# A newly searched order of the steps behind the first MoE product, in a fused scan and MoE kernel

## The chip, the cores and the metric

The kernel runs on one core of a Trainium2 chip. The metric is the device time of one execution in microseconds. In the text PE is the tensor engine (PEld its weight loads), DVE the vector engine, ACT the scalar engine, POOL the GpSimd engine, SP the sync engine, which issues nearly all transfers here. PSUM is the memory into which PE writes, SBUF the working memory.

## The reference

Two parts follow each other. The first is a gated state-space scan over `x` (4 batches, 8 heads, 768 positions, 32 wide), with decay `a` and the projections `B` and `C` (16 states). The second is a feed-forward layer over its 3072 tokens of 256 values, with 2048 inner values and a tanh-GELU. All inputs and the output are float32.

```
for each chunk of the sequence:
    cum    = cumsum(log(clip(a)))
    M      = (C B^T) * exp(cum_i - cum_j), lower triangle
    y      = M x  +  (C state) * exp(cum)
    state  = exp(sum) * state + sum_j B_j x_j exp(cum_end - cum_j)
out = gelu_tanh(y_as_tokens @ w_in) @ w_out        # 256 -> 2048 -> 256
```

## The kernel before

The sequence is cut into 24 chunks of 128 positions (six for each batch). Two chunks are a unit `u`, so there are 12 units of 256 tokens. The whole program is a set of named steps, each with a fixed engine. The text `ORDERED` names every step once, and the program issues them in exactly this order. An engine works through its own steps in the order of the text and waits only where data or a buffer isn't ready. A letter behind a colon moves a step to another engine (`:A` ACT, `:D` DVE, `:P` POOL, `:S` SP), `~n` and `+n` put n blocks of matmuls with zeros in a place where PE would stand still.

The steps of a unit or a chunk, with the lines that the profile gives:

- `load_*` (SP): `load_wi.q`, `load_wo.q` bring quarters of the weights, `load_bc.b.i` the B and C of batch b (i = 1 is C), `load_bc1.i` those of chunks 4 and 5, `load_x.u` the x of a unit. `wi.q.k` and `wo.q.k` (line 325 on POOL, 327 on DVE, 323 on ACT) convert the weights to bf16.
- `R`, `tp2`, `tp6.q`, `recip1`, `recip.1.4` (DVE; lines 340, 351, 383, 391) make the decay factors of chunks 4 and 5, and of batches 1 to 3; `pe`, `pp`, `pend` (lines 394 to 396, 402) the factors between chunks.
- `mul1.i` (line 444), `T1.i` (452), `bh1`, `ce1.e` (461), `N1` (472), `bn1` prepare B and C of chunks 4 and 5: scaling, transposing on PE, evicting. For batch 1 these are `mul.1.i` (484), `T.1.i` (493), `E.1.i`, `F.1` (two instructions, 523), `N.1` (529) and `bn.1`. For batches 2 and 3 the transposing goes through DRAM (`load_wr`, `load_tr`, `load_bn`), and only `mul.b.i` and `F.b` remain.
- `G.u` (603) gives the products C B^T of a unit in two PSUM pairs `ga`, `gb`; `M.u.0` and `M.u.1` (613, DVE) mask `ga` and `gb` into `m`. `castx.u` converts x. `D.u` (636) gives the state's increments into a buffer of the pool `hp`; `S.u.k` (682, 684, DVE) adds them to the state, and `SP.c` (691, DVE) spreads the state of chunk c for PE.
- `Y.u` (658, 667) gives y in the PSUM bank `yb`; `yev.u` evicts it into `xm`. From unit 3 on `Y.u` also holds `D` and `G` of the unit behind it.
- `s1.u.i` (717, PE) is an eighth of the first MoE product: four matmuls into one of the two `hp` buffers. `gelu.u.i` (721, ACT) empties that buffer. `s2.u.k.q` (735, PE) is a quarter of the second product for half a unit: four matmuls into the one bank `o_ps` (for a few chunks at the end into `yb`). `oev.c` (323 on ACT, 327 on DVE) evicts chunk c, and `store.c` writes it.

Limits that tie the order together are the buffers: two of `hp` (shared by `s1`, `D`, `pp`), one `o_ps`, one `ga`, one `gb`, one `yb`, six for outputs. `ga` holds the transposed B in its second bank too, so `G` waits until `bn1` or `bn.1` has emptied it:

```
        tn[1].takes("gb", e1)
        tn[0].takes("ga", e0)
        nn.takes("ga", bb)
```

Of the kernel before, what the change touches and what calls it, by code (L numbers as in the profile page):

```python
# [32 lines left out]
s1.2.6 M.3.0 gelu.2.5 wo.3.0:D gelu.2.6 s2.0.0.2.o castx.4.None s1.2.7 Y.3 gelu.2.7 wo.3.1:D
s2.0.1.2.o S.4.0 yev.3.0.2 S.4.1 s2.0.0.3.o oev.0 load_x.5 s1.3.0 s1.3.1 mul.2.1 s2.0.1.3.o
load_wr.2.1 load_x.6 gelu.3.0 gelu.3.1 s1.3.2 oev.1:D SP.8 s1.3.3 s2.1.0.0.o gelu.3.2 M.4.0
gelu.3.3 SP.7 s2.1.0.1.o s2.1.0.2.o s2.1.0.3.o oev.2:D s1.3.4 s1.3.5 s2.1.1.0.o gelu.3.4 M.4.1
mul.2.0:P castx.5.None:A s2.1.1.1.o Y.4 S.5.0 s2.1.1.2.o load_wr.2.0 s2.1.1.3.o load_tr.2.1
load_bn.2 oev.3:D gelu.3.5 s1.3.6 s1.3.7 s2.2.0.0.o yev.4.0.2 load_tr.2.0 gelu.3.6 s1.4.0 SP.9
M.5.1 gelu.3.7 s2.2.0.1.o store.0 store.2 gelu.4.0 s1.4.1 castx.6.None:A s1.4.2 SP.10 s2.2.0.2.o
load_x.7 s2.2.0.3.o gelu.4.1 oev.4:D gelu.4.2 s1.4.3 s1.4.4 load_bc.3.1 s2.2.1.0.o s2.2.1.1.o  # L40
s2.2.1.2.o gelu.4.3 gelu.4.4 s2.2.1.3.o s1.4.5 oev.5 s1.4.6 gelu.4.5 M.5.0 s2.3.0.0.o F.2 store.1
Y.5 s2.3.0.1.o s2.3.0.2.o yev.5.0.2 gelu.4.6 s2.3.0.3.o s1.4.7 S.6.0 gelu.4.7 load_bc.3.0 S.6.1
store.3 s1.5.0 oev.6:D SP.12 s2.3.1.0.o gelu.5.0 s1.5.1 s2.3.1.1.o gelu.5.1 castx.7.None:A
mul.3.1:P s2.3.1.2.o s1.5.2 gelu.5.2 M.6.1 s2.3.1.3.o s1.5.3 M.6.0 Y.6 oev.7:D S.7.0 gelu.5.3
load_x.8 s1.5.4 S.7.1 s2.4.0.0.o s2.4.0.1.o s1.5.5 SP.13 gelu.5.4 load_wr.3.1 yev.6.0.2
castx.8.None store.4 load_x.9 gelu.5.5 SP.14 s2.4.0.2.o s2.4.0.3.o oev.8 s1.5.6 s1.5.7 mul.3.0
castx.9.None s2.4.1.0.o gelu.5.6 load_wr.3.0 gelu.5.7 M.7.0 s2.4.1.1.o s1.6.0 M.7.1 load_tr.3.1
Y.7 S.8.0 load_tr.3.0 gelu.6.0 s1.6.1 s1.6.2 s2.4.1.2.o gelu.6.1 yev.7.0.2:D gelu.6.2 s2.4.1.3.o
oev.9:D M.8.0 s1.6.3 gelu.6.3 SP.16 s1.6.4 s2.5.0.0.o s1.6.5 gelu.6.4 gelu.6.5 M.8.1 SP.15
s2.5.0.1.o s1.6.6 load_bn.3 s2.5.0.2.o s1.6.7 gelu.6.6 s2.5.0.3.o s1.7.0 oev.10:D gelu.6.7 s1.7.1  # L50
gelu.7.0 s2.5.1.0.o s1.7.2 store.5 gelu.7.1 s2.5.1.1.o gelu.7.2 s1.7.3 gelu.7.3 s1.7.4 gelu.7.4
store.9 F.3 s2.5.1.2.o s1.7.5 s1.7.6 gelu.7.5 s2.5.1.3.o s1.7.7 gelu.7.6 store.6 Y.8 oev.11
yev.8.0.2:D gelu.7.7 S.9.0 load_x.10 s2.6.0.0.o s2.6.0.1.o s2.6.0.2.o S.9.1 s1.8.0 gelu.8.0
s2.6.0.3.o s1.8.1 gelu.8.1 oev.12:D s1.8.2 gelu.8.2 s2.6.1.0.o castx.10.None:D store.10 store.11
store.7 s1.8.3 gelu.8.3 s2.6.1.1.o s1.8.4 gelu.8.4 s1.8.5 s2.6.1.2.o s2.6.1.3.o SP.18 M.9.1
gelu.8.5 s1.8.6 M.9.0 store.8 oev.13 gelu.8.6 Y.9 store.12 s2.7.0.0.o s2.7.0.1.o S.10.0 s2.7.0.2.o
yev.9.0.2:D s2.7.0.3.o S.10.1 s1.8.7 oev.14 s1.9.0 load_x.11 castx.11.None:A gelu.8.7 M.10.0
s2.7.1.0.o s2.7.1.1.o SP.21 s1.9.1 s2.7.1.2.o s2.7.1.3.o gelu.9.0 SP.20 gelu.9.1 oev.15 s1.9.2
M.10.1 SP.19 gelu.9.2 Y.10 s1.9.3 gelu.9.3 store.15 S.11.0 s1.9.4 M.11.0 s2.8.0.0.o s1.9.5
gelu.9.4 store.14 s2.8.0.1.o gelu.9.5 s2.8.0.2.o SP.22 s2.8.0.3.o s1.9.6 store.13 gelu.9.6  # L60
oev.16:D s1.9.7 gelu.9.7 yev.10.0.2:D s2.8.1.0.o s1.10.0 s2.8.1.1.o s1.10.1 gelu.10.0 s1.10.2
s2.8.1.2.o gelu.10.1 s1.10.3 s2.8.1.3.o M.11.1 oev.17:D gelu.10.2 s1.10.4 store.17 gelu.10.3
s1.10.5 Y.11 yev.11.0.2:D gelu.10.4 s2.9.0.0.o s1.10.6 gelu.10.5 s2.10.0.0.yb s2.9.0.1.o
s2.10.0.1.yb s1.10.7 s2.10.0.2.yb s2.9.0.2.o gelu.10.6 s2.9.0.3.o s1.11.0 gelu.10.7 s1.11.1 oev.18
s2.9.1.0.o gelu.11.0 store.16 s2.10.0.3.yb s1.11.2 s2.9.1.1.o oev.20 gelu.11.1 s2.9.1.2.o
gelu.11.2 s1.11.3 s2.9.1.3.o gelu.11.3 oev.19:D s1.11.4 s1.11.5 s2.11.0.0.yb gelu.11.4 s1.11.6
gelu.11.5 s2.10.1.0.o store.20 s1.11.7 gelu.11.6 s2.11.0.1.yb s2.10.1.1.o s2.10.1.2.o store.19
s2.10.1.3.o gelu.11.7 oev.21:D s2.11.0.2.yb s2.11.0.3.yb s2.11.1.0.o oev.22:D s2.11.1.1.o store.22
# [915 lines left out]
```

## Time and profile before

| | |
|---|---|
| time, median of 3 runs | 118.44 us (117.72, 118.44, 118.59) |
| profiled execution, span from first to last instruction | 116.9 us |
| what the runs' median has beyond that span | 1.5 us |
| granted TensorE clock in the profile | 1.000 |
| PE, ACT, DVE, POOL busy | 110.1, 72.1, 69.4, 21.4 us |
| first MoE matmul, last MoE matmul | starts at 12.5 us, ends at 113.9 us |
| read from and written to HBM | 11.04 MB, 3.93 MB |

The profile shows one execution; the profiler gives its span alone, and its own time with what lies around the span is not among the three runs. Ends of matmuls are modelled: a group of four that takes PE 0.44 us is shown with 0.60, because the last one outlasts its slot. Gaps between PE's groups are therefore read from starts. A row of the timeline holds start, length, engine, line, operation, output and inputs with their shapes, and a count of merged instructions; brackets hold the idle time of the engine ahead of it and who ended it.

### The profile page before, as it was taken

The numbers are of one execution on the slowest core, as the hardware profiler recorded it, in microseconds if no ns is written. First come the engines' busy times: TensorE is split into PE (matmuls) and PEld (weight loads), VectorE is DVE, ScalarE is ACT, GpSimd is POOL, SyncE is SP. The second block draws the span as 40 slices with busy tenths as digits, with TensorE's granted clock in tenths as the row PEclk, the third lists the DMA queues.
The fourth block names the chain that finished last, engine by engine and source line by source line (L and its number), as shares of the span: only waits on it lengthen the run. The fifth ranks groups of instructions, "written<-read, shape, count | busy, mean of one in ns | idle before, by whom it ended". The sixth has DMA issues, their size and how long they took to land.

```text
span 116.9 us, 3379 instructions
## 1 busy us (share of the span) xinstructions
PE 110.1 (94%) x1426; PEld 92.0 (79%) x1426; DVE 69.4 (59%) x140; ACT 72.1 (62%) x139; POOL 21.4 (18%) x38
## 2 busy tenths in 40 slices
...
PEclk9999999999999999999999999999999999999999
...
GB/s 26 228 332 357 281 252 178 208 288 257 305 143 90 185 47 219 213 253 200 72 25 171 121 163 63 0 140 98 40 6 63 71 0 52 43 0 50 45 47 132
DMA packets 43007, 15.97 MB, mean 137 GB/s; under 512 B 36657, under 2 KB 41457, under 8 KB 42993
## 3 DMA queue, kind: packets, MB, share of 16 engines
...
q8 instruction: 11, 0.18, 0.6%
q10 hardware_dynamic: 192, 0.13, 0.5%
...
HBM read 11.04 MB, written 3.93 MB: 128 GB/s over the span
## 4 chain that ended last, share of the span: by engine, by line
PE 75%; DMA 8%; DVE 6%; SPq 6%; issue 2%; POOL 1%; ACT 0%; DVEq 0%; POOLq 0%
PE o_ps L735 33%; PE hp L717 30%; DMA bcf<-in_B_dram 8%; PE yb L735 3%; SPq L190 3%; PE ga L603 3%; PE yb L658 2%; DVE m L613 2%; PE yb L667 2%; DVE ce L523 1%; SPq L150 1%; DVE bh L327 1%; DVE bc L484 1%; SPq L159 1%; SPq L183 1%
## 5 line engine op out<-in xcount | busy, mean ns | idle before, releaser
L721 ACT ACTIVATE gT<-hp 128x512 bf16<-128x512 f32 x96 | 54.3, 596 | 25.0 <-PE hp L717 24.6
L717 PE MATMUL hp<-xm,w_in_sb 128*128 128x256 bf16 x384 | 53.3, 273 | 0.6 <-ACT gT L721 0.4
L735 PE MATMUL o_ps<-w_out_sb,gT 128*128 128x256 bf16 x352 | 47.3, 273 | 0.0
L717 PEld LDWEIGHTS <-w_in_sb 128*128 128x128 bf16 x384 | 41.4, 114 | 3.5 <-issue 1.9
L735 PEld LDWEIGHTS <-gT 128*128 128x128 bf16 x384 | 37.0, 98 | 4.9 <-issue 1.1
L327 DVE COPY o_sb<-o_ps 128x256 f32<-128x256 f32 x13 | 5.5, 425 | 23.8 <-PE o_ps L735 20.4
L613 DVE TENSOR_TENSOR m<-ga,tri 128x1024 bf16<-128x1024 f32 x12 | 14.6, 1218 | 0.1
L613 DVE TENSOR_TENSOR m<-gb,tri 128x1024 bf16<-128x1024 f32 x11 | 13.4, 1219 | 0.7 <-PE gb L603 0.7
L323 ACT ACTIVATE o_sb<-o_ps 128x256 f32<-128x256 f32 x9 | 3.5, 385 | 9.2 <-PE o_ps L735 9.2
L705 PE MATMUL yb<-wz 128*128 128x512 bf16 (+3 forms) x23 | 7.6, 481 | 1.1 <-DVE wz L220 1.1
L691 DVE SCALAR_TENSOR_TENSOR sp_new<-s_new,pend,bmask 128x256 bf16<-128x256 f32 x17 | 7.9, 476 | 0.0
L327 DVE CAST xm<-yb 128x512 bf16<-128x512 f32 x6 | 4.1, 687 | 5.8 <-PE hp L636 4.8
L684 DVE SCALAR_TENSOR_TENSOR s_new<-s_new,pend,hp 128x64 f32<-128x64 f32 x13 | 3.6, 279 | 6.4 <-PE hp L636 6.2
L705 PEld LDWEIGHTS <-wz 128*128 128x128 bf16 x26 | 3.0, 120 | 5.1 <-issue 3.2
L667 PE MATMUL yb<-m,x 128*32 128x128 bf16 x192 | 6.1, 220 | 0.0
L603 PE MATMUL ga<-ce,bh 32*128 32x256 bf16 x48 | 4.7, 273 | 1.3 <-DVE bn L327 0.9
L484 POOL TENSOR_TENSOR bc<-bc_t,pt 128x768 bf16<-128x768 f32 x2 | 3.0, 1494 | 13.8 <-DMA bc_t<-in_C_dram 13.7
L658 PE MATMUL yb<-ce,sp_new 128*32 128x128 bf16 x160 | 5.3, 221 | 0.0
L603 PE MATMUL gb<-ce,bh 32*128 32x256 bf16 x48 | 4.7, 273 | 0.0
L735 PE MATMUL yb<-w_out_sb,gT 128*128 128x256 bf16 x32 | 4.6, 273 | 0.0
L667 PEld LDWEIGHTS <-x 128*32 128x32 bf16 x192 | 3.8, 97 | 0.8 <-issue 0.8
L323 ACT ACTIVATE xm<-yb 128x512 bf16<-128x512 f32 x6 | 3.6, 595 | 1.1 <-PE hp L636 1.1
...
## 6 DMA issues: line engine op xcount, KB each, us to landing
...
```

What stands on the lines that cost most here:

```text
L323: nc.scalar.activation(o, i, AF.Copy)
L327: nc.vector.tensor_copy(out=o, in_=i)
L484: (nc.gpsimd if eng == "POOL" else nc.vector).tensor_tensor(out=d["bc16"][:, i], in0=d["bc"].rearrange("p i h (r n) -> p i r h n", r=R6)[: ...
L603: nc.tensor.matmul(out=gbank(g)[:, 256 * k:256 * k + 256], lhsT=bh_of(2 * u + k)[gs], rhs=ce_of(2 * u + k)[gs], start=True, stop=True, til ...
L613: nc.vector.tensor_tensor(out=m_of(u)[:, 2 * i:2 * i + 2].rearrange("p g k e t -> p (g k e) t"), in0=gx[i].rearrange("p g (k t) -> p (g k) ...
L658: nc.tensor.matmul(out=y4[32 * j:32 * j + 32, k, w], lhsT=sp[:, 32 * h:32 * h + 32], rhs=ce_of(gc)[:, h % 2], start=first(j), stop=False, ...
L667: nc.tensor.matmul(out=y4[32 * j:32 * j + 32, k, w], lhsT=X16[u][:, k, 32 * h:32 * h + 32], rhs=m[:, h // 2, h % 2, :], start=first(j), st ...
L691: nc.vector.scalar_tensor_tensor(out=sp_new.rearrange("p (g d) -> p g d", g=4), in0=(XN[0][:, H * D:H * D + 64] if gc == 0 else state[("s" ...
L705: nc.tensor.matmul(out=t[:, 0:m * 128], lhsT=wz, rhs=w3.to_broadcast([128, m, 128]), start=True, stop=True, skip_group_check=True)
L717: nc.tensor.matmul(out=hp[:, j * T:(j + 1) * T], lhsT=w_in_k[:, w, q, k], rhs=xm[:, w, u * T:(u + 1) * T], start=(w == 0), stop=(w == 1))
L721: nc.scalar.activation(gts[u][:, 2 * i:2 * i + 2], hps.pop((u, i)).rearrange("p (j t) -> p j t", j=2), AF.Gelu_apprx_tanh)
L735: nc.tensor.matmul(out=ops[gc], lhsT=gts[u][:, fi, k * Q:(k + 1) * Q], rhs=w_out_sb[:, fi, :], start=(fi == 0 and (u > 0 or k == 0)), stop ...
```

## The change

Only the text `ORDERED` is altered. The set of steps is the same. All steps as far as `s1.0.0` stay as they are, apart from `c_wz`, which is named ahead of four loads on other queues. The order of the transfers on SP, stores among them, is the same name for name. Behind `s1.0.0` the order on PE, DVE, ACT and POOL is new, and 38 steps are on another engine. The ten filling blocks of `s1.1.3+10` are left out. Core of the diff:

```diff
-load_aq.0 load_aq.1 load_aq.2 load_aq.3 c_wz load_bc0.1 c_ident c_m4 c_sel c_tri c_zero load_bc0.0
+c_wz load_aq.0 load_aq.1 load_aq.2 load_aq.3 load_bc0.1 c_ident c_m4 c_sel c_tri c_zero load_bc0.0
...
-load_wi.3 S.1.0 s1.0.0 SP.1 xn.2 load_bc1.1 wi.2.0 gelu.0.0 G.1 s1.0.1 s1.0.2 M.1.1 M.1.0
-load_bc1.0 load_wo.0 wi.3.0:D gelu.0.1 wi.2.1 s1.0.3 load_x.2 SP.2 pe wi.3.1 gelu.0.2 load_bc.1.1
-gelu.0.3 tp6.2 s1.0.4 load_bc.1.0 gelu.0.4 load_x.3 load_wo.1 xn.3 s1.0.5 s1.0.6 Y.1 gelu.0.5 pp
-tp2 gelu.0.6 tp6.3 recip1 s1.0.7 S.1.1 yev.1.0.2 mul1.0:P mul1.1:P tp6.1 pend gelu.0.7 s1.1.0
-wo.0.1 T1.0 s1.1.1 T1.1 gelu.1.0 bh1 N1 gelu.1.1 s1.1.2 tp6.0 s1.1.3+10 bn1 ce1.1 load_wo.2
-castx.2.None SP.3 wo.0.0 ce1.0 gelu.1.2 gelu.1.3 G.2 s1.1.4 recip.1.4 s1.1.5 gelu.1.4 M.2.1
-mul.1.1:P s2.0.0.0.o D.2 M.2.0 load_x.4 gelu.1.5 s2.0.1.0.o s1.1.6 T.1.1 gelu.1.6 S.2.0 s1.1.7
-SP.4 Y.2 mul.1.0 yev.2.0.2:D gelu.1.7 wo.1.0 wo.1.1 T.1.0 E.1.1:A castx.3.None:A s1.2.0 wo.2.0
-s1.2.1 E.1.0 wo.2.1 load_wo.3 load_bc.2.1 N.1 gelu.2.0 F.1 s1.2.2 bn.1:D G.3 gelu.2.1 gelu.2.2 D.3
...
+S.1.0 s1.0.0 xn.2 gelu.0.0 load_bc1.1 wi.2.0 G.1 wi.2.1 xn.3 tp2 s1.0.1 M.1.0 s1.0.2 gelu.0.1 recip1
+M.1.1 s1.0.3 wi.3.0 SP.1 mul1.1:P gelu.0.2 s1.0.4 S.1.1 gelu.0.3 gelu.0.4 SP.2 pe T1.1 load_bc1.0
+s1.0.5 tp6.3 wi.3.1 load_wo.0 s1.0.6 Y.1 ce1.1 mul1.0:P gelu.0.5 gelu.0.6 load_x.2 pp T1.0 ce1.0:D
+yev.1.0.2 s1.0.7 bh1 pend:D gelu.0.7 s1.1.0 tp6.1 tp6.0 tp6.2 N1 s1.1.1 bn1:D wo.0.1 G.2 gelu.1.0
+load_bc.1.1 gelu.1.1 s1.1.2 castx.2.None wo.0.0 s1.1.3 gelu.1.2 recip.1.4 mul.1.1:P M.2.1 gelu.1.3
+load_bc.1.0 s1.1.4 s2.0.0.0.o M.2.0 gelu.1.4 D.2 T.1.1 s1.1.5 S.2.0 SP.3 gelu.1.5 s1.1.6 SP.4
+load_x.3 E.1.1 Y.2 mul.1.0:P T.1.0 s1.1.7 load_wo.1 gelu.1.6 yev.2.0.2:D gelu.1.7 s2.0.1.0.o s1.2.0
+s1.2.1 E.1.0 N.1 F.1 wo.1.0:A gelu.2.0 wo.1.1 s2.0.0.1.o bn.1:D gelu.2.1 s1.2.2 castx.3.None:D
+gelu.2.2 load_wo.2 load_x.4 G.3 D.3 wo.2.0 S.3.0 s2.0.1.1.o wo.2.1:D SP.6 s1.2.3 s2.0.0.2.o S.3.1
+s2.0.1.2.o gelu.2.3 M.3.0 s1.2.4 load_wo.3 s1.2.5 wo.3.0:A wo.3.1 s2.0.0.3.o M.3.1 s2.0.1.3.o
+load_bc.2.1 oev.0:D castx.4.None gelu.2.4 gelu.2.5 s1.2.6 Y.3 oev.1 s2.1.0.0.o gelu.2.6 s2.1.0.1.o
+s2.1.0.2.o yev.3.0.2 SP.7 S.4.0 s2.1.0.3.o M.4.1 S.4.1 mul.2.1:P s1.2.7 oev.2 s1.3.0 s2.1.1.0.o
+s2.1.1.1.o s2.1.1.2.o gelu.2.7 s2.1.1.3.o s1.3.1 oev.3:D M.4.0 gelu.3.0 gelu.3.1 s1.3.2 s2.2.0.0.o
...
+gelu.4.5 oev.7:D s1.4.6 s2.4.0.0.o gelu.4.6 Y.5 S.6.0 load_bc.3.0 store.3 s1.4.7 yev.5.0.2 S.6.1
+mul.3.1 load_x.8 load_wr.3.1 s2.4.0.1.o s1.5.0 mul.3.0:P gelu.4.7 s2.4.0.2.o castx.7.None:D gelu.5.0
+store.4 s1.5.1 gelu.5.1 s2.4.0.3.o s1.5.2 oev.8:D load_x.9 load_wr.3.0 gelu.5.2 s1.5.3 s2.4.1.0.o
...
+gelu.6.2 s1.6.4 gelu.6.3 s2.5.1.3.o gelu.6.4 s1.6.5 castx.8.None gelu.6.5 store.6 oev.11:D Y.7 F.3
+load_x.10 s1.6.6 gelu.6.6 s2.6.0.0.o S.8.0 s1.6.7 store.10 gelu.6.7 yev.7.0.2:D store.11 s2.6.0.1.o
+s1.7.0 s2.6.0.2.o M.8.0 M.8.1 SP.16 s1.7.1 s2.6.0.3.o gelu.7.0 oev.12:D s1.7.2 gelu.7.1 s1.7.3
...
```

Both texts run on in this manner to the last step; the second MoE products come earlier against the first ones in the new order (at `Y.3` three more of them have been issued and one `s1` step less).

More of the change, by code (lines that the diff above doesn't have):

```diff
@@ L33 @@
[L33 to L68, printed above, removed]
@@ L69 @@
-s2.11.1.2.o store.21 s2.11.1.3.o oev.23 store.18 store.23
+load_wi.2 SP.0 ~17 Y.0 wi.0.1:A wi.0.0:A S.0.0 yev.0.0.2 wi.1.1 XX.1 wi.1.0:A R XD.1 S.0.1 load_wi.3
+S.1.0 s1.0.0 xn.2 gelu.0.0 load_bc1.1 wi.2.0 G.1 wi.2.1 xn.3 tp2 s1.0.1 M.1.0 s1.0.2 gelu.0.1 recip1
+M.1.1 s1.0.3 wi.3.0 SP.1 mul1.1:P gelu.0.2 s1.0.4 S.1.1 gelu.0.3 gelu.0.4 SP.2 pe T1.1 load_bc1.0
+s1.0.5 tp6.3 wi.3.1 load_wo.0 s1.0.6 Y.1 ce1.1 mul1.0:P gelu.0.5 gelu.0.6 load_x.2 pp T1.0 ce1.0:D
+yev.1.0.2 s1.0.7 bh1 pend:D gelu.0.7 s1.1.0 tp6.1 tp6.0 tp6.2 N1 s1.1.1 bn1:D wo.0.1 G.2 gelu.1.0
```

30 lines of the change are left out of this document (27 added, 3 removed).

## The prediction

> **What bounds the kernel now.** I read the page's busy times first, then the stages, then the engines' timelines where the stages show idle time. Two lines of the page (busy us, share, instructions; granted TensorE clock in 40 slices):
>
> ```profile
> PE 110.1 (94%) x1426; PEld 92.0 (79%) x1426; DVE 69.4 (59%) x140; ACT 72.1 (62%) x139; POOL 21.4 (18%) x38
> PEclk9999999999999999999999999999999999999999
> ```
>
> Four rows of the stages (stretch, length, busy us of PE, PEld, DVE, ACT, POOL, clock, DMA share, GB/s):
>
> ```profile
> 20.00:25.00 5.00, 4.98 (x54) 3.93 (x55) 4.42 (x7) 3.84 (x9) 3.26 (x4) 1.00 1.13 221
> 25.00:30.00 5.00, 3.82 (x70) 2.81 (x67) 4.64 (x7) 3.89 (x7) 3.07 (x5) 1.00 1.07 298
> 30.00:35.00 5.00, 5.00 (x88) 4.30 (x85) 4.33 (x10) 3.36 (x6) 0.00 (x0) 1.00 0.98 210
> 105.00:110.00 5.00, 5.00 (x49) 4.71 (x47) 0.42 (x1) 3.89 (x8) 0.00 (x0) 1.00 0.18 56
> ```
>
> TensorE is full from 30 us to the end at full clock, so behind 30 us an order can only lose; it can win where PE is not full. In the rows from 25 to 30 us DVE is the fuller engine (4.64 of 5). The timeline says what PE waits for (start, length, instruction, in brackets idle time before it and who ended it):
>
> ```profile
> 28.21 0.60 PE L717 MATMUL hp<-xm,w_in_sb 128*128 128x256 bf16 x4
> 29.69 0.28 PE L603 MATMUL ga<-ce,bh 32*128 32x256 bf16 x2 [0.89 <-DVE bn L327]
> 24.82 0.48 DVE L691 SCALAR_TENSOR_TENSOR sp_new<-s_new,pend,bmask 128x256 bf16<-128x256 f32 x1
> 25.22 0.95 DVE L484 TENSOR_TENSOR bc<-bc_t,rt 128x768 bf16<-128x768 f32 x1
> 26.14 0.69 DVE L327 CAST xm<-yb 128x512 bf16<-128x512 f32 x1
> 26.78 0.96 DVE L327 COPY bh<-ga 128x768 bf16<-128x768 bf16 x1
> 27.65 1.52 DVE L523 TENSOR_SCALAR ce<-ch,par 128x768 bf16<-128x768 bf16 x2
> 29.09 0.54 DVE L327 COPY bn<-ga 128x768 bf16<-128x768 bf16 x1
> ```
>
> G.3 (29.69) is the last long wait of PE, and it waits for an unbroken DVE chain: SP.4, mul.1.0, yev.2, E.1.0, both halves of F.1, bn.1. So the change is worth what it does to the moment of G.3, plus the products that PE has done by then, minus new waits behind it.
>
> **The change part by part.** Moving `c_wz` to the front alters no queue, as it already led DVE. The order on SP is word for word the same, and none of its issues before load_wr.2.1 waits for an engine, so landings up to about 35 us stay. The rest goes into four terms.
>
> *One more product before G.3.* Before G.3 the new order has s2.0.0.1 besides all that stood there. PE takes 0.44 us for four matmuls (the starts 43.13 and 44.01 below are eight apart): **−0.44**. The ten filling blocks of `s1.1.3+10` go; their place is one third matmul row,
>
> ```profile
> 20.62 0.70 PE L705 MATMUL hp<-wz 128*128 128x512 bf16 x3
> ```
>
> 0.54 us if the 0.16 by which a matmul outlasts its slot (0.60 for four slots of 0.44) is taken off. They filled a wait, so I count them as room and not as gain: PE could stand at G.3 at 28.21 + 0.44 + 0.44 − 0.54 = 28.55, about 28.7 with its mode switch. That is the earliest G.3.
>
> *The DVE chain up to G.3.* Rows for what leaves and what comes:
>
> ```profile
> 13.48 1.23 DVE L613 TENSOR_TENSOR m<-gb,tri 128x1024 bf16<-128x1024 f32 x1 [0.17 <-PE gb L603]
> 14.62 1.22 DVE L613 TENSOR_TENSOR m<-ga,tri 128x1024 bf16<-128x1024 f32 x1
> 15.75 0.42 DVE L327 CAST w_in_sb<-wf 128x512 bf16<-128x512 f32 x1
> 16.08 0.48 DVE L691 SCALAR_TENSOR_TENSOR sp_new<-s_new,pendq,bmask 128x256 bf16<-128x256 f32 x1
> 16.93 1.94 DVE L351 STREAM_TRANSPOSE rt<-r_t 32x192 f32<-32x192 f32 x6
> 22.24 1.23 DVE L613 TENSOR_TENSOR m<-gb,tri 128x1024 bf16<-128x1024 f32 x1 [0.55 <-PE gb L603]
> 18.14 0.19 ACT L323 ACTIVATE pend<-hp 128x24 f32<-128x24 f32 x1
> 20.47 0.38 ACT L323 ACTIVATE bn<-ga 128x256 bf16<-128x256 bf16 x1
> 20.73 0.84 ACT L461 ACTIVATE ce<-gb,par 128x256 bf16<-128x256 bf16 x2
> 26.06 0.81 ACT L323 ACTIVATE ch<-gb 128x768 bf16<-128x768 bf16 x1
> ```
>
> Idle time 0.17 and 0.55 goes, because tp2 and then M.1.0 fill the first and M.2.1 stands behind DVE work alone. Off DVE go wi.3.0 (15.75 to 16.08: 0.33) and mul.1.0 (25.22 to 26.14: 0.92). Onto DVE come ce1.0, pend, bn1 and E.1.1. DVE does none of these here; ACT's rows give 0.42, 0.19, 0.38 and 0.81. E.1.1 has the shape of E.1.0, 26.78 to 27.65, so 0.87; a 256-wide eviction takes a DVE slot of 0.34 (43.33 to 43.68 in the last fence and its neighbour's start); so 0.34 + 0.20 + 0.34 + 0.87 = 1.75, bounds 1.5 and 2.0. castx.3, too, but behind bn.1, beside G.3. F.1 is the fourth item. It ran while POOL was casting; F.2, the same two instructions, ran with POOL idle:
>
> ```profile
> 48.73 0.74 DVE L523 TENSOR_SCALAR ce<-ch,par 128x768 bf16<-128x768 bf16 x2
> 27.67 1.29 POOL L325 CAST w_out_sb<-wf 128x512 bf16<-128x512 f32 x2 [0.23 <-DMA wf<-in_moe_w_out_dram]
> ```
>
> In the new order one cast of w_out goes to ACT and one to DVE, so F.1 costs nearer 0.74 than 1.52: −0.78. Sum: −0.72 − 1.25 + 1.75 − 0.78 = −1.00, G.3 at 28.7, just where PE could be.
>
> *POOL in DVE's way.* The three SP (two operands in SBUF) now meet POOL. Rows:
>
> ```profile
> 7.75 8.91 DMA bcf<-in_B_dram
> 12.91 2.04 POOL L325 CAST w_in_sb<-wf 128x512 bf16<-128x512 f32 x3 [0.33 <-DMA wf<-in_moe_w_in_dram]
> 19.80 0.61 POOL L325 CAST w_out_sb<-wf 128x512 bf16<-128x512 f32 x1
> 20.35 0.86 POOL L325 CAST x<-x_t 128x512 bf16<-128x512 f32 x1
> 21.88 1.49 POOL L484 TENSOR_TENSOR bc<-bc_t,pt 128x768 bf16<-128x768 f32 x1
> 20.30 0.43 DVE L691 SCALAR_TENSOR_TENSOR sp_new<-s_new,pend,bmask 128x256 bf16<-128x256 f32 x1
> 35.28 2.01 POOL L484 TENSOR_TENSOR bc<-bc_t,rt 128x768 bf16<-128x768 f32 x1 [5.31 <-DMA bc_t<-in_B_dram]
> 34.99 0.95 DVE L484 TENSOR_TENSOR bc<-bc_t,pt 128x768 bf16<-128x768 f32 x1
> ```
>
> DVE: today SP.1 stands between S.1.0 and the 0.17 of idle, so S.1.0 ends near 13.48 − 0.17 − 0.40 = 12.9. Then tp2 takes 0.9 (four of the six transposes of 16.93), M.1.0 and M.1.1 1.14 each (13.48 to 14.62), recip1 and S.1.1 some 0.2 each (estimates), so SP.1 is due at 16.3 and SP.2 at 16.9. POOL: three casts to 14.95, mul1.1 at 15.2 behind recip1, wi.3.1 then until 16.5, mul1.0 at its landing 16.66 (7.75 + 8.91) until 17.3. So SP.1 meets wi.3.1 with 0.2 left and SP.2 meets mul1.0 with 0.4 to 0.5. M.2.1 is due at 21.7 (22.24 less 0.72, 0.33 and SP.3's slot of 0.36, plus 0.88 for ce1.0, pend and bn1); SP.3, now behind two M and S.2.0, at 24.2; mul.1.1 and mul.1.0 occupy POOL from 21.7 for 2 × 1.49, to 24.7: 0.5 left. What a meeting costs DVE no SP row shows outright. Nothing, by the row at 20.30: 0.43, with a POOL cast from 19.80 to 20.41 in progress, but with its last 0.11 us only. By F.1 against F.2, (1.52 − 0.74)/2 = 0.39 each. At most about 0.7 each, if the pushed chain pushes mul.1.1 too. POOL pays the same way: 2.01 against 1.49 when mul.2.1 was running on DVE first, 0.86 against 0.61 beside SP.3. I take F.1's 0.39, three times: **+1.17**, bounds 0 and 2.0, and G.3 at 29.87, **+0.18** on today's 29.69.
>
> The Trainium skill (SBUF — State Buffer, Who interferes with whom) says that a VectorE instruction with two SBUF inputs and a GpSimd instruction that reads SBUF exclude each other, and that whoever starts first keeps the port for its whole instruction. By that rule the three meetings would cost 0.2 + 0.45 + 0.5 = 1.15, nearly what I took. F.1 and the 2.01 row agree with it; the 20.30 row is no test.
>
> *Behind G.3.* PE must stay full. castx.3 on DVE (0.42, as the 15.75 cast) ends as PE reaches D.3. wo.2.1 on DVE and wo.3.0 on ACT come 0.1 to 0.4 before their products. M.3.1, 0.3 before Y.3; if SP.6 meets POOL this goes. mul.2.1 moves to POOL, which is free when C lands, and is followed there by mul.2.0. mul.3.1 goes from POOL to DVE behind S.6.1, some 3 us later, and load_wr.3.1 blocks store.4 and load_x.9 on SP for that time; by counting 0.44 us steps, the first reader (F.3) and the sixth-next output buffer have over 2 us left. The turns of the one `o_ps` bank are the tightest:
>
> ```profile
> 42.25 1.05 PE L735 MATMUL o_ps<-w_out_sb,gT 128*128 128x256 bf16 x8
> 43.13 1.04 PE L717 MATMUL hp<-xm,w_in_sb 128*128 128x256 bf16 x8
> 44.01 0.60 PE L735 MATMUL o_ps<-w_out_sb,gT 128*128 128x256 bf16 x4
> 43.33 0.42 DVE L327 COPY o_sb<-o_ps 128x256 f32<-128x256 f32 x1 [0.98 <-PE o_ps L735]
> 43.68 0.48 DVE L691 SCALAR_TENSOR_TENSOR sp_new<-s_new,pend,bmask 128x256 bf16<-128x256 f32 x1
> ```
>
> Two s1 steps between, and the eviction ends at 43.75, 0.25 before the bank is written again. The new order uses the same spacing; in it oev.12 alone stands behind a full DVE stretch (F.3, S.8.0, yev.7, M.8.0, M.8.1, SP.16) and comes out level with PE: **+0.05**, bounds 0 and 0.4. The tail (eviction, last store) is unchanged.
>
> *Sum:* −0.44 + 0.18 + 0.05 = −0.21. The profiled span is 116.9, so I forecast 116.7; the median of the runs is 118.44, 1.5 above that span, and the same distance makes **118.2**. Its own range, by 0.3 either way at the meetings and 0.4 of the runs' spread (117.72 to 118.59): 117.6 to 118.8.
>
> **The rivals.**
> *POOL does not hold up DVE.* For it: the 20.30 row. Against it: F.1. Then G.3 comes at 28.7, the gain is 0.99 + 0.44 − 0.05 = 1.38 and the time 117.1.
> *PE becomes late before G.3.* The new order lets PE wait for SP.2 in Y.1, for pend behind tp6.3 and ce1.0 before s1.1.0, and for bn1 behind three transposes (0.5 each) before G.2. Then G.2 comes at 21.3, and 12 steps of 0.44 with about 2.4 for G.2, D.2, Y.2 and eighteen transposes follow: 29.0. If in addition the gelus and SP.3 stop it for 1.2 to 1.4, G.3 comes at 30.3: 118.44 + 0.6 − 0.44 + 0.1 = 118.7. Against it: ACT loses four evictions there.
> *Evictions late on DVE (slower).* oev.3, 6, 7, 8, 12 and 13 are on DVE with two s1 steps to the next writing. From 0.25 us of delay each stops PE. An eviction that meets an M half way is 0.61 late, 0.36 beyond its margin; six make 2.2: 120.4. For it: DVE is handed casts and mul.3.1, and its order was fixed by an estimate. Against it: the same spacing costs nothing at 43.33, and DVE is idle before that.
>
> **How the numbers follow.** Forecast 0.42, POOL harmless 0.20, PE late 0.18, evictions late 0.20. Faster by over 1% (under 117.26; about what a measurement here can tell from no change) needs nearly all of the harmless case: 0.16, and 0.04 from cheaper evictions: 0.20. Slower by over 1% (over 119.62): most of the last rival, 0.18, and 0.04 of unseen waits: 0.22. The rest, 0.58, within 1%. The range reaches from the harmless case less 0.2 to about the middle of the last one: 116.9 to 119.7, with 1 in 10 left out on either side.
>
> **What would show it.** Right: s2.0.0.1 before G.3; G.3 between 29.5 and 30.2; SP.1 to SP.3 longer than 0.48 or late behind POOL; F.1 under 1.0; PE full after 31 us. Wrong: G.3 before 29.2 (POOL harmless), idle PE of over 0.3 us in a stretch behind 35 us with an o_sb eviction as releaser (last rival), or a load that lands over 0.5 us later than it does today.

## The result, and the profile after

After takes 119.12 us in the median (118.49 to 120.68, 22 runs) against 118.45 (117.72 to 119.12, 22 runs) before: ratio 1.0055, 95% interval 1.0034 to 1.0076, so 0.67 us slower where 0.2 less was forecast. That lies in the range and in the band of 1%, but the time went up and not down. The profiled execution of after has a span of 117.8 us and a time of 119.47. Two lines of its page, and five stages (stretch, length, busy us of PE, PEld, DVE, ACT, POOL, granted clock, DMA share, GB/s):

```profile
PE 109.4 (93%) x1423; PEld 91.9 (78%) x1423; DVE 69.6 (59%) x139; ACT 71.5 (61%) x136; POOL 24.4 (21%) x42
PEclk9999999999999999999999999999999999999999
```

```profile
16.00:20.00 4.00, 2.89 (x54) 2.33 (x54) 3.80 (x10) 3.07 (x8) 2.57 (x5) 1.00 0.95 224
20.00:25.00 5.00, 4.16 (x46) 3.21 (x45) 4.91 (x9) 3.23 (x6) 3.17 (x4) 1.00 1.05 193
25.00:30.00 5.00, 4.45 (x73) 3.82 (x72) 5.00 (x9) 3.10 (x6) 2.34 (x3) 1.00 1.01 271
30.00:35.00 5.00, 5.00 (x57) 4.14 (x54) 4.48 (x9) 2.88 (x6) 2.62 (x3) 1.00 1.07 268
105.00:110.00 5.00, 5.00 (x48) 4.73 (x47) 0.43 (x1) 3.41 (x7) 0.00 (x0) 1.00 0.17 56
```

PE is full from 30 us on, as before; DVE is full from 20 to 30 us, where before left it 0.9 us idle. The timeline of after, first the instructions that were to be watched on DVE, then POOL beside them, then PE at its waits and at G.3:

```profile
16.10 0.47 DVE L689 SCALAR_TENSOR_TENSOR sp_new<-s_new,pendq,bmask 128x256 bf16<-128x256 f32 x1
16.68 0.65 DVE L689 SCALAR_TENSOR_TENSOR sp_new<-s_new,pendq,bmask 128x256 bf16<-128x256 f32 x1
17.26 0.56 DVE L392 TENSOR_TENSOR pe<-ac,r_t 64x3 f32<-64x3 f32 x1
17.92 0.50 DVE L394 TENSOR_TENSOR pe<-pe,m 64x24 f32<-64x24 f32 x1
24.92 1.69 DVE L689 SCALAR_TENSOR_TENSOR sp_new<-s_new,pend,bmask 128x256 bf16<-128x256 f32 x2
28.86 1.09 DVE L521 TENSOR_SCALAR ce<-ch,par 128x768 bf16<-128x768 bf16 x2
16.43 0.62 POOL L442 TENSOR_TENSOR bc0s<-bcf,pt 128x256 bf16<-128x256 f32 x1 [0.47 <-DMA bcf<-in_C_dram]
17.00 0.80 POOL L323 CAST w_in_sb<-wf 128x512 bf16<-128x512 f32 x1
17.77 0.62 POOL L442 TENSOR_TENSOR bc0s<-bcf,rt 128x256 bf16<-128x256 f32 x1
24.44 1.50 POOL L482 TENSOR_TENSOR bc<-bc_t,rt 128x768 bf16<-128x768 f32 x1 [0.26 <-DMA bc_t<-in_B_dram]
17.11 0.29 PE L450 MATMUL gb<-ident,bc0s 128*128 128x128 bf16 x2 [1.24 <-POOL bc0s L442]
21.58 0.28 PE L601 MATMUL ga<-ce,bh 32*128 32x256 bf16 x2 [0.47 <-DVE bn L325]
26.27 0.29 PE L656 MATMUL yb<-ce,sp_new 128*32 128x128 bf16 x8 [0.55 <-DVE sp_new L689]
27.00 0.51 PE L491 MATMUL ga<-ident,bc 128*128 128x128 bf16 x6
30.47 0.28 PE L601 MATMUL ga<-ce,bh 32*128 32x256 bf16 x2
```

For comparison, SP.2 and the two instructions of `pe` in the timeline of before:

```profile
16.08 0.48 DVE L691 SCALAR_TENSOR_TENSOR sp_new<-s_new,pendq,bmask 128x256 bf16<-128x256 f32 x1
16.48 0.15 DVE L394 TENSOR_TENSOR pe<-ac,r_t 64x3 f32<-64x3 f32 x1
16.73 0.18 DVE L396 TENSOR_TENSOR pe<-pe,m 64x24 f32<-64x24 f32 x1
```

G.3 comes at 30.47, 0.78 later than before, not 0.18. From G.3 to the end of the last matmul it is 83.70 us against 84.18: the product done ahead is worth its 0.44, and nothing is lost behind G.3. So the matmuls end 0.3 us later (114.2 against 113.9). DVE is held up where POOL runs: SP.2 by 0.17, the two of `pe` by 0.41 and 0.32, SP.3 with SP.4 by 0.81 (1.69 against the 0.88 that the first experiment with a short mul.1.0 shows below), F.1 by 0.35 over F.2's 0.74. SP.3 alone takes 1.30 and ends 0.28 us after POOL's mul.1.0. Together that is 2.06 us on DVE's chain, which would else have reached G.3 at 28.4. Not all of it could have been won: bn.1, the last of the chain, ends at 30.41, and PE, which waited 0.55 us for SP.4 ahead of Y.2, runs from there (26.27) to G.3 without a wait of over 0.2 us, so it would have been the next bound.

The span is 0.9 us longer and the matmuls only 0.3. The rest lies behind the last store's landing: 0.89 us of span before (116.01 to 116.9), 1.40 after (116.36 to 117.76). The waits of SP, from 114 us on, show it in their last line (engine, line, what it waited for: us in total, times, longest). Before:

```profile
SPq L979 <- DMA out_dram<-o_sb: 1.1, 2, 0.7
SPq L979 <- PEq L979: 0.6, 2, 0.4
```

After:

```profile
SPq L977 <- DMA out_dram<-o_sb: 1.1, 2, 0.7
SPq L977 <- PEq L977: 1.1, 2, 0.9
```

These are the program's closing instructions, in which all engines wait for each other. POOL is the late one: its last drain starts at 117.35 in after, 0.38 us after the instruction in front of it has ended; in before that gap is 0.03. What lies between span and time goes the other way, 1.71 us after and 1.96 (median of 137 later runs, 1.77 to 2.12) before. From last landing to the time that makes 3.11 against 2.85: 0.26 us in which no step of the order runs.

### The profile page after: what moved, and what is told of

It is laid out like the page before. It is cut to its first block, busy times and chain, and to the rows that moved or that the text cites. A ratio compares the mean times of both kernels' runs of the same rounds, so it can differ in the third digit from the quotient of the medians.

```text
span 117.8 us, 3373 instructions
## 1 busy us (share of the span) xinstructions
PE 109.4 (93%) x1423; PEld 91.9 (78%) x1423; DVE 69.6 (59%) x139; ACT 71.5 (61%) x136; POOL 24.4 (21%) x42
## 4 chain that ended last, share of the span: by engine, by line
PE 75%; DMA 8%; DVE 5%; SPq 5%; ACT 2%; issue 1%; POOL 1%; ACTq 0%; POOLq 0%
PE o_ps L733 33%; PE hp L715 31%; DMA bcf<-in_C_dram 8%; PE yb L733 3%; SPq L188 3%; PE yb L656 2%; PE ga L601 2%; PE yb L665 2%; DVE m L611 2%; DVE rt L349 1%; DVE sp_new L689 1%; ACT gT L719 1%; SPq L148 1%; SPq L181 1%; SPq L157 1%
## 5 line engine op out<-in xcount | busy, mean ns | idle before, releaser
L689 DVE SCALAR_TENSOR_TENSOR sp_new<-s_new,pend,bmask 128x256 bf16<-128x256 f32 x17 | 8.5, 527 | 0.1
L323 POOL CAST x<-x_t 128x512 bf16<-128x512 f32 x6 | 3.7, 615 | 19.9 <-PE gb L601 17.1
L482 POOL TENSOR_TENSOR bc<-bc_t,rt 128x768 bf16<-128x768 f32 x3 | 4.5, 1496 | 12.7 <-DMA bc_t<-in_B_dram 12.7
L321 ACT ACTIVATE xm<-yb 128x512 bf16<-128x512 f32 x9 | 5.4, 597 | 1.4 <-PE hp L634 1.4
L656 PEld LDWEIGHTS <-sp_new 128*32 128x32 bf16 x160 | 2.9, 96 | 2.4 <-issue 1.4
```

The lines of the kernel that those rows point to most:

```text
L321: nc.scalar.activation(o, i, AF.Copy)
L482: (nc.gpsimd if eng == "POOL" else nc.vector).tensor_tensor(out=d["bc16"][:, i], in0=d["bc"].rearrange("p i h (r n) -> p i r h n", r=R6)[: ...
L656: nc.tensor.matmul(out=y4[32 * j:32 * j + 32, k, w], lhsT=sp[:, 32 * h:32 * h + 32], rhs=ce_of(gc)[:, h % 2], start=first(j), stop=False, ...
L689: nc.vector.scalar_tensor_tensor(out=sp_new.rearrange("p (g d) -> p g d", g=4), in0=(XN[0][:, H * D:H * D + 64] if gc == 0 else state[("s" ...
```

## The experiments

The kernel before ran beside each of them; ratios are to it, with 95% intervals.

**Which half of the order?** Two mixed orders, joined behind D.3.

```diff
 e1: before's text up to D.3, then after's steps in after's order
+... G.3 gelu.2.1 gelu.2.2 D.3 s2.0.0.1.o S.3.0 s2.0.1.1.o SP.6 s1.2.3 s2.0.0.2.o S.3.1 ...
 e2: after's text up to D.3, then before's steps in before's order
+... load_x.4 G.3 D.3 wo.2.0 wo.2.1 load_wo.3 load_bc.2.1 s1.2.3 S.3.0 S.3.1 load_bc.2.0 ...
```

> The old order up to D.3 and the new order behind it (s2.0.0.1 comes right behind D.3; wo.2.0 and wo.2.1 stay on POOL). Theory A (the loss lies ahead of G.3: DVE instructions that read two SBUF operands, and F.1, stand still while POOL reads): G.3 near 29.7 us as in the kernel before, SP.3 under 0.5 us, time within 0.3% of the kernel before. Rival B (the loss lies behind G.3, in the new order of the rest): still slower by 0.5 to 0.7 us. Rival C (late landing of the C of chunks 4 and 5 stops PE at T1.1): as A, since the old front has T1.1 later.

> The new order up to D.3 and the old order behind it. Theory A: G.3 near 30.4 us, SP.3 near 1.3 us, and slower than the kernel before by 0.3 to 0.8 us. Rival B: within 0.2 us of the kernel before. Rival C: as A, with PE idle for over 1 us ahead of T1.1.

e1: 1.0068 (1.0030 to 1.0105). e2: 1.0100 (1.0059 to 1.0141). Both are slower than before. Of e1's 0.7% some 0.3% is the long end of the span that is treated below (3.08 us from the last landing to the time); e2 doesn't have it (2.60). In e2 G.3 is 16.95 us behind G.1, PE waits another 0.4 behind 36 us, and the matmuls from G.3 on take 84.40 us, 0.70 more than after's; why this mixture is worse than the whole new order stays open. In e1 the front is as good as before's, and PE waits behind G.3 instead, for casts of the last quarter of w_out:

```profile
32.84 0.63 ACT L323 ACTIVATE w_out_sb<-wf 128x512 bf16<-128x512 f32 x1 [0.72 <-DMA wf<-in_moe_w_out_dram]
32.88 0.61 POOL L325 CAST w_out_sb<-wf 128x512 bf16<-128x512 f32 x1 [2.86 <-DMA wf<-in_moe_w_out_dram]
33.53 1.03 PE L735 MATMUL o_ps<-w_out_sb,gT 128*128 128x256 bf16 x8 [0.28 <-ACT w_out_sb L323]
```

e6 takes that wait away by loading the quarter one place earlier:

```diff
-... load_x.4 ... load_wo.3 ...
+... load_wo.3 load_x.4 ...
```

> The first experiment's order (old up to D.3, new behind it) with load_wo.3 ahead of load_x.4 on SP. Theory D (behind G.3 the new order uses the last quarter of w_out 2 to 3 us earlier than the old one, and its landing at 30.8 us in the profile of before was an early one): PE's wait ahead of s2.0.0.3, 0.45 us at 33 us in the first experiment, goes, and the time falls by 0.3 to 0.6 us against it, to within 0.3% of the kernel before. If the loss of the first experiment lies elsewhere: no change.

1.0024 (0.9987 to 1.0060). The same product, now without a wait:

```profile
32.48 1.04 PE L735 MATMUL o_ps<-w_out_sb,gT 128*128 128x256 bf16 x8
```

So the new rest uses the last quarter early (32.48 in e6, about 35.1 in before, behind Y.3), at times before it has landed. In the whole new order this doesn't show, because G.3 is late.

**What makes G.3 late?** e3 takes PE's wait before T1.1 (1.24 us above) out of the new order.

```diff
-... SP.2 pe T1.1 load_bc1.0 ... Y.1 ce1.1 mul1.0:P ... pp T1.0 ce1.0:D yev.1.0.2 s1.0.7 bh1 ...
+... SP.2 pe load_bc1.0 ... Y.1 mul1.0:P ... pp T1.1 T1.0 ce1.0:D yev.1.0.2 s1.0.7 ce1.1 bh1 ...
```

> The new order with T1.1 on PE moved behind pp (just ahead of T1.0) and ce1.1 on ACT moved behind yev.1, so that PE does not stop for mul1.1 between s1.0.4 and s1.0.5. Theory A: PE is a microsecond less late at s1.0.5, but DVE sets G.3, so G.3 stays within 0.15 us of 30.4 and the time within 0.2 us of the new order. Rival C: G.3 comes 0.4 us or more earlier and the time falls by 0.4 us or more.

1.0036 (1.0003 to 1.0069): some 0.2 us better than after, which the intervals don't tell from nothing. PE waits at other places in its stead (0.47 us for wi.3.1's cast and 0.47 for `pe`), G.3 is at 30.25, and DVE still meets POOL:

```profile
25.06 1.41 DVE L691 SCALAR_TENSOR_TENSOR sp_new<-s_new,pend,bmask 128x256 bf16<-128x256 f32 x2
```

e9 shortens what SP.3 waits for and leaves the order alone. Its mul.1.0 multiplies a third of its columns, and T.1.0 reads that third three times; the other two thirds of the scaled B are left out.

```diff
-            out=d["bc16"][:, i], ...
+            out=d["bc16"][:, i, 0:k], ...          # k = 2 of 6 for mul.1.0
-            ... in_=bc[:, i, r], identity=ident)
+            ... in_=bc[:, i, r % 2 if (b, i) == (1, 0) else r], identity=ident)
```

> The new order; POOL's mul.1.0 multiplies only a third of its columns (256 of 768), and T.1.0 reads that third three times, so the instruction should take about 0.55 us in place of 1.50 and SP.3 should no longer wait for it. Theory (DVE held up by POOL's reads decides the moment of G.3): SP.3 takes 0.48 to 0.6 in place of 1.30, G.3 comes 0.6 to 0.8 sooner than in the new order (29.7 to 29.9), ratio to before 0.999 to 1.001. Rival (TensorE's own wait before T1.1 and G.2 decides, the DVE wait only lies over it): SP.3 is as short, but G.3 moves by under 0.3 and the ratio stays at 1.004 to 1.007. Where wi.3 and C come late, yev.2 waits for PE and part of the gain goes.

```profile
24.13 0.62 POOL L485 TENSOR_TENSOR bc<-bc_t,rt 128x256 bf16<-128x256 f32 x1
24.91 0.88 DVE L692 SCALAR_TENSOR_TENSOR sp_new<-s_new,pend,bmask 128x256 bf16<-128x256 f32 x2
29.67 0.28 PE L604 MATMUL ga<-ce,bh 32*128 32x256 bf16 x2
```

0.9997 (0.9966 to 1.0027). SP.3 and SP.4 take 0.88 in place of 1.69, G.3 comes 0.80 sooner, and the time is back at before's, with an end of the span as long as after's (3.09 us). Up to SP.3 the two profiles agree: G.2 comes at 21.57 (21.58 in after) and SP.3 starts at 24.91 (24.92). So PE's waits ahead of G.2 are still there, and they did not decide. (mul.1.0 had ended at 25.94 in after and T.1.0 read it at 27.00, so a sooner end of mul.1.0 was no gain by itself.)

e10 does e3 and e9 together.

> As the run before, with T1.1 behind T1.0 and ce1.1 ahead of bh1 as well, so that neither suspected wait is left before G.3. Theory that DVE alone decides: about the same as the run before, 0.998 to 1.001. Rival that each of the two holds the other half: clearly faster than either alone, ratio 0.994 to 0.998, G.3 at 29.2 to 29.5.

1.0014 (0.9976 to 1.0053), no more than e9 alone. G.3 came at 29.44, and now the wait of e1 appears:

```profile
33.75 0.92 PE L736 MATMUL o_ps<-w_out_sb,gT 128*128 128x256 bf16 x7 [0.85 <-ACT w_out_sb L323]
```

Two attempts to take SP.3 out of POOL's way by the order failed. e5 puts SP.3 behind bn1; e7 does that, and lets PE and DVE of the front change places as well; e8 is e7 with load_wo.3 ahead of load_x.4.

```diff
 e5:
-... bn1:D ... recip.1.4 ... S.2.0 SP.3 gelu.1.5 s1.1.6 SP.4 load_x.3 E.1.1 ...
+... bn1:D SP.3 ... recip.1.4 ... S.2.0 E.1.1 gelu.1.5 s1.1.6 SP.4 load_x.3 ...
 e7, besides SP.3 and e3's edit:
-... SP.2 pe ... tp6.3 wi.3.1 ... Y.2 mul.1.0:P T.1.0 s1.1.7 ... yev.2.0.2:D ... E.1.0 N.1 ...
+... SP.2 ... tp6.3 pe ... wi.3.1:A ... mul.1.0:P ... s1.1.7 T.1.0 E.1.0 Y.2 ... yev.2.0.2:A ... N.1 ...
```

> The new order with two steps of DVE moved: SP.3 directly behind bn1, where POOL stands still, and E.1.1 ahead of SP.4, so that both SP run outside mul.1.0. Theory A (POOL blocks DVE): SP.3 falls from 1.0 to 1.3 us to 0.5, SP.4 stays near 0.48, bn.1 ends 0.3 to 0.6 us earlier than in the new order and the time falls by 0.2 to 0.5 us. If SP.3 were long for a cause of its own, it stays over 1 us in its new place.

> The new order with its front freed of what blocked DVE: T1.1 and ce1.1 later as in the third experiment, wi.3.1 on ACT, pe behind tp6.3, SP.3 behind bn1, E.1.1 ahead of SP.4, T.1.0 and E.1.0 ahead of Y.2 and yev.2, and yev.2 on ACT. Theory A: pe, SP.3 and SP.4 at their undisturbed lengths, G.3 0.7 to 1.3 us earlier than in the new order (29.2 to 29.8), time 118.0 to 118.5, at or under the kernel before, less what a late w_out costs (theory D: up to 0.5). Rival B (loss behind G.3): no more than 0.2 us of gain.

> The freed front with load_wo.3 ahead of load_x.4. Theories A and D together: 0.2 to 0.5 us under the freed front, 117.7 to 118.1, faster than the kernel before by 0.3 to 0.6%. Theory A without D: as the freed front.

e5: 1.0072 (1.0029 to 1.0115); e7: 1.0120 (1.0071 to 1.0169); e8: 1.0116 (1.0063 to 1.0169). SP.3 takes 0.48 in the profiles of e5 and e7, and it did not help. e7 shows where its gain went: `pe` was put off, PE waits for it, and DVE then waits for PE.

```profile
18.91 0.37 PE L402 MATMUL hp<-pe,selp 128*128 128x24 f32 x2 [0.92 <-DVE pe L396]
19.44 0.48 DVE L463 TENSOR_SCALAR ce<-gb,par 128x256 bf16<-128x256 bf16 x1 [0.67 <-PE gb L452]
```

e5's profile can't be used for that: it is of an execution of 121.76 us (its median is 119.65), in which the loads came late (wi.3 at 16.7 and C at 17.1, where the others have 13.9 to 15.4 and 14.4 to 16.6). Its loss is not explained. So that SP.3 costs time is shown by e9 alone.

e4 tested F.1 in the old order: both halves of wo.2 go from POOL to ACT.

```diff
-... s1.2.0 wo.2.0 s1.2.1 E.1.0 wo.2.1 ... gelu.2.2 D.3 ... gelu.2.3 ...
+... s1.2.0 s1.2.1 E.1.0 ... gelu.2.2 wo.2.0:A D.3 ... gelu.2.3 wo.2.1:A ...
```

> The old order with the two conversions wo.2.0 and wo.2.1 moved from POOL to ACT (behind gelu.2.2 and gelu.2.3), so that POOL converts nothing while DVE does F.1. Theory A: the halves of F.1 fall from 0.84 and 0.76 us to 0.41 each, G.3 comes 0.6 to 0.75 us earlier (29.0), the time falls by 0.5 to 0.8 us to about 117.8. If F.1 were long for a cause of its own: no change.

```profile
27.49 0.95 DVE L523 TENSOR_SCALAR ce<-ch,par 128x768 bf16<-128x768 bf16 x2
```

0.9980 (0.9948 to 1.0011). F.1 takes 0.95 against 1.52 and G.3 stands 16.1 us behind G.1 against 16.7, but the time is hardly less. The profile of before was an unlucky draw at this place: with the same steps in the same order, e13 and e18 below have G.3 16.3 us behind G.1, and F.1 takes 1.10 in both.

e11 was meant to beat both kernels: e6, with mul.1.0 on POOL and wo.2 on ACT.

```diff
-... SP.4 Y.2 mul.1.0 ... wo.2.0 s1.2.1 E.1.0 wo.2.1 ... gelu.2.1 gelu.2.2 D.3 ...
+... SP.4 mul.1.0:P Y.2 ... s1.2.1 E.1.0 ... gelu.2.1 wo.2.0:A gelu.2.2 wo.2.1:A D.3 ...
```

> A version meant to beat both: the old order up to D.3 with the new one behind it and load_wo.3 ahead of load_x.4 (the run e6), and two items taken off the DVE chain before G.3: mul.1.0 goes to POOL, where it follows mul.1.1 (about 23.4 to 24.9, so SP.4 at 24.8 meets only its end), and both halves of wo.2 go to ACT behind gelu.2.1 and gelu.2.2, so that F.1 meets no cast. Theory: DVE is freed by 0.9 + 0.5, G.3 then hangs on PE alone, 28.3 to 28.7, and the ratio is 0.993 to 0.997. Rival: B's chunk lands later than 24.4, SP.4 waits for POOL and the gain is gone: 0.999 to 1.003; or wo.2 on ACT comes late for s2.0.0.2 and shows as a PE wait at 31 us.

0.9991 (0.9957 to 1.0024). DVE is free as planned (0.83 us idle ahead of yev.2), G.3 is 15.9 us behind G.1, and the time is no better. That led back to the end of the span.

**The end of the span.** e11 has the same 3.11 us between last landing and time as after. In every profile with a long end the late instruction of POOL is the 69th that the trace holds of it. The three positions that occur, and before (us behind the last landing):

```
                  recorded on POOL   late one starts    instruction in front of it ended
before                  65           none in the span   -
e7                      70           69th, at 1.04      0.66
after                   71           69th, at 0.99      0.61
e1                      73           69th, at 0.72      0.33
```

e12 to e14 leave every step alone and add small instructions to POOL at its last step, when it has nothing left to do.

```diff
-            fill(yb, int(w[1:]))
+        if w[0] == "!":                       # "!12" stands at the end of ORDERED
+            for _ in range(int(w[1:])):
+                nc.gpsimd.memset(cz[:, 0, 0, 0, 0:2], 0.0)
```

> The new order with 12 tiny memsets on POOL behind its last step, at about 55 us, where POOL has nothing left to do. They change no other engine. Theory (the 69th recorded instruction of POOL is late, wherever it stands; in the new order it is a drain of the closing sequence): the late place is passed long before the end, the span ends 0.9 us behind the last landing in place of 1.40, the distance from span to time stays at 1.7, and the time falls by 0.4 to 0.5: ratio to before 1.001 to 1.003. Rival (the late drain has to do with what the new order does last): 1.40 stays and the ratio stays at 1.004 to 1.007.

> The kernel before with 6 of these memsets, which bring POOL from 65 recorded instructions to 71, as many as the new order has. Theory: the late place moves into the closing sequence: 1.40 behind the last landing in place of 0.89, distance from span to time 1.7 in place of 2.0, time +0.2: ratio 1.001 to 1.002. Rival: nothing moves, 0.89 and 2.0.

> The kernel before with 16 memsets. Theory: the late place is passed in POOL's idle time: 0.89 behind the last landing and 1.7 from span to time, so 0.3 us less: ratio 0.997 to 0.998. Rival: no change, 0.999 to 1.001.

The new order with 12 more: 1.0002 (0.9973 to 1.0031). The old one with 6: 1.0028 (1.0001 to 1.0054); with 16: 0.9970 (0.9939 to 1.0000). Each moved the way the theory said; the first two lie 0.1% outside the ranges that it gave (1.001 to 1.003 and 1.001 to 1.002), well within the noise. The last line of SP's waits moves with it; the new order with 12:

```profile
SPq L981 <- PEq L981: 0.6, 2, 0.4
```

and the old order with 6:

```profile
SPq L983 <- PEq L983: 1.1, 2, 0.9
```

From last landing to time it is 2.64 in e12, 3.10 in e13 and 2.63 in e14, where after has 3.11 and before 2.85. (e14's profile is of an execution of 120.21 us, with its median at 118.07; only this part of it is used here.) In e12, where POOL's 69th recorded instruction is a memset, it starts 0.06 us behind the one before it, like its neighbours: the lateness shows only where the 69th is one of the closing instructions. e18 repeats e14:

> The kernel of e14 once more. If the 0.3 us are real: ratio 0.996 to 0.999, the span 0.9 us behind the last landing and 1.7 us from span to time. If e14 was an accident of its chip: 0.999 to 1.002.

0.9983 (0.9956 to 1.0010), again with 2.65 behind the last landing. Its F.1:

```profile
27.72 1.10 DVE L524 TENSOR_SCALAR ce<-ch,par 128x768 bf16<-128x768 bf16 x2
```

Three more versions were meant to beat both kernels. e15 is e11 with s2.0.1.0 behind T.1.0, s2.0.0.1 ahead of G.3, and 12 memsets; e16 is e4 with 18; e17 is e16 with mul.1.0 on POOL.

```diff
 e15:
-... gelu.1.5 s2.0.1.0.o s1.1.6 ... T.1.0 E.1.1:A ... bn.1:D G.3 ... D.3 s2.0.0.1.o S.3.0 ...
+... gelu.1.5 s1.1.6 ... T.1.0 s2.0.1.0.o E.1.1:A ... bn.1:D s2.0.0.1.o G.3 ... D.3 S.3.0 ...
```

> A version meant to beat both: the run e11, with s2.0.1.0 moved behind T.1.0 (so that PE has it to do while yev.2 runs, where e11 waits 0.5 us) and s2.0.0.1 ahead of G.3 (where e11 waits 0.3), and with the 12 memsets. Expected if both causes are as stated: G.3 15.9 to 16.3 us behind G.1 with one product more done than in e11, so 0.5 us less than e11, and 0.4 less behind the last landing: ratio to before 0.991 to 0.995. If the moves only shift the waits, the memsets alone leave 0.995 to 0.997.

> The run e4 (old order, both halves of wo.2 on ACT) with 18 memsets on POOL: G.3 16.1 us behind G.1 in place of 16.7, and 2.63 us in place of 2.9 from the last landing to the time. If G.3 counts in full: 0.5 and 0.27 less, ratio 0.993 to 0.995. If G.3's gain is lost again behind it: 0.997, as e14.

> As the run before, and mul.1.0 on POOL behind mul.1.1: DVE is free of 0.9 us ahead of G.3, which then hangs on PE: 15.9 us behind G.1. If G.3 counts in full: ratio 0.991 to 0.994. If B lands late (past 24.4) SP.4 waits for POOL and it equals the run before.

e15: 0.9976 (0.9945 to 1.0008); e16: 0.9988 (0.9957 to 1.0019); e17: 0.9985 (0.9954 to 1.0015). All three were expected at 0.991 to 0.995; all are better than after, and none shows more than the 0.3 us that POOL's drain is worth. Part of the reason is the yardstick: against the 16.3 us of e13 and e18, and not before's 16.7, G.3 of e4, e11 and e16 (16.1, 15.9, 15.9 behind G.1) is only 0.1 to 0.3 sooner, and their matmuls from G.3 on take 0.1 to 0.2 longer (84.28 to 84.34). In e17 mul.1.1 waited for a late C, mul.1.0 followed it at 24.42, and SP.4 waited for that:

```profile
24.42 1.50 POOL L485 TENSOR_TENSOR bc<-bc_t,rt 128x768 bf16<-128x768 f32 x1
24.99 1.21 DVE L692 SCALAR_TENSOR_TENSOR sp_new<-s_new,pend,bmask 128x256 bf16<-128x256 f32 x1
```

The best that the runs support is the old order with 16 memsets: 0.997 and 0.998 in two sets, each with an interval that reaches 1.000 or 1.001.

## Why the prediction was wrong

Two steps failed: the term "POOL in DVE's way", which listed three instructions of DVE where more were held up, and "the same distance" from span to time. The terms one by one.

**The sum.** With the closing instructions alike, the order alone costs 0.3 us: after against e13 is 1.0055 to 1.0028 (both 3.1 us behind the last landing), e12 against e14 and e18 is 1.0002 to 0.9977 (all 2.6). The other 0.3 us of the 0.67 are the closing instructions: e13 measures them at 0.28% with the old order. Each of these differences carries 0.3 to 0.4% of uncertainty, so neither pair alone is clear of zero; that both agree is what supports the split. The profiles of before and after give parts of the same size (0.78 − 0.48 at G.3, 0.26 at the end).

**The product before G.3**, −0.44: right, 0.48 to 0.49 in the profiles (84.18 against 83.70 in after, 83.69 in e12).

**The DVE chain**: G.3 at 28.7 without POOL; by DVE alone after gives 28.4 (30.47 − 2.06). Right to 0.3, for DVE; how soon PE could have been there no run shows.

**POOL in DVE's way** is the term that failed: +1.17 for three SP was taken, within bounds of 0 and 2.0, and 2.06 was measured. The three SP are nearly right in sum (0, 0.17 and 0.81, together 0.98), but by luck: SP.1 paid nothing, and SP.3 paid twice the 0.39. The two multiplies on POOL were taken to run from 21.7 to 24.7. But mul.1.1 waits for recip.1.4, which stands on the same pushed DVE chain, and starts at 22.69; mul.1.0 waits for B until 24.44 and ends at 25.94, so that 1.02 us of it is left when SP.3 comes, and not 0.5. What was left out is `pe` (0.41 + 0.32), which was moved into the same 2 us of POOL's casts and never costed, and F.1, whose −0.78 counted on a POOL without casts and was 0.35 too much. The three errors, −0.19, +0.73 and +0.35, with the −0.3 of the chain, are the 0.6 us by which G.3 came later than forecast. In e9, one meeting less (0.81) brought 0.80 at G.3 and 0.6% in the time; `pe` and F.1 were not taken out of the new order by themselves.

The Trainium skill (SBUF — State Buffer, Who interferes with whom) says that a VectorE instruction with two SBUF inputs and a GpSimd instruction that reads SBUF contend, and that such a lock is held for the whole instruction. The traces agree: SP.3 lasted until 0.28 us after mul.1.0, and tiny `pe` (64x3) took 0.56 in place of 0.15. Read as a rule for every two-input instruction in POOL's busy time, it would have put `pe` on the list. F.1 multiplies one tensor by a column of factors and is no such instruction; that a POOL cast holds it up, its own rows show (1.09 in after, 0.74 with POOL idle).

**Behind G.3**, +0.05: right; PE has no wait of over 0.1 us there, and the rival of late evictions didn't occur. Only e1 and e10 show that the room was borrowed: with G.3 sooner, the last quarter of w_out is late.

**From span to time.** "The same distance" of 1.5 us was taken as fixed; it isn't, and it set the span of one execution against the median of others, where span and time of the same execution lie 1.96 apart in before and 1.71 in after. The part of the span behind the last landing had no term, since no step of the diff lies there. 0.26 us came in at this place.

**The rival "PE late before G.3"** had its waits (1.24 before T1.1, 0.47 before G.2), but G.2 came at 21.58 against 21.69, e3 gains some 0.2, within the noise, and in e9 G.3 followed DVE with G.2 unmoved; DVE was the bound. **POOL harmless** is out.

**Landings.** C for chunks 4 and 5 landed at 14.7 in before's profile and at 16.3 in after's (the POOL row at 16.43), though nothing on SP ahead of it was changed; over all profiles 14.4 to 17.1. A load over 0.5 us late was among the signs of being wrong. With an early landing (14.5) the same steps have G.3 at 29.79, where 29.87 was forecast (e12):

```profile
16.88 0.65 DVE L690 SCALAR_TENSOR_TENSOR sp_new<-s_new,pendq,bmask 128x256 bf16<-128x256 f32 x1
17.70 0.41 DVE L395 TENSOR_TENSOR pe<-pe,m 64x24 f32<-64x24 f32 x1
24.60 1.40 DVE L690 SCALAR_TENSOR_TENSOR sp_new<-s_new,pend,bmask 128x256 bf16<-128x256 f32 x2
28.25 0.91 DVE L522 TENSOR_SCALAR ce<-ch,par 128x768 bf16<-128x768 bf16 x2
29.79 0.28 PE L602 MATMUL ga<-ce,bh 32*128 32x256 bf16 x2
```

POOL costs DVE about 1.2 us there (SP.1 0.08, SP.2 0.17, `pe` 0.23, SP.3 with SP.4 0.52, F.1 0.17), against 2.06 in after. The yardstick was a draw too: F.1's saving of 0.78 was taken from the 1.52 in before's profile, and with the 1.10 of e13 and e18 it could be 0.36 at most. From G.1 to the end of the last matmul it is 100.84 us in before, 100.45 in e13 and 100.43 in e18 with the old order, and 101.37 in after and 100.57 in e12 with the new (in after G.1 comes 0.2 sooner than in before). So one pair of profiles gives the order's loss as 0.53 and another as 0.14; only the medians of the runs, 0.3, stand for it. The signs named beforehand (G.3 between 29.5 and 30.2, F.1 under 1.0) were set tighter than one execution can tell.
